# Reordering loads and work at the layer change of a two-layer cached-attention decode kernel, with a rebuilt final projection

## The chip, the cores and the metric

The kernel runs on one core of one Trainium2 chip. The metric is device time in microseconds (us). The kernel before took 547.49 us in the median of its first 4 runs (547.14 to 548.09).

A "page" is the summary of one profiled execution; the other views are answers to questions put to the same trace. Engines: PE is the matrix engine, PEld its weight loads, DVE the vector engine, ACT the scalar engine, POOL the general engine. SP is the engine that issues the loads here, and SPq its queue.

## The reference

One token goes through attention, a gated feed-forward network, and then both again. Both layers have the **same** weights and the same caches.

```
x = A_x                                    # 1 x 1 x 640
x = x + attention(layernorm(x), k_cache, v_cache, wq, wo)
x = x + ffn(layernorm(x), w1, w3, w2)
x = x + attention(layernorm(x), k_cache, v_cache, wq, wo)   # same operands
x = x + ffn(layernorm(x), w1, w3, w2)
# attention: 32 heads of width 192, the last 4096 of 32768 cached positions
# ffn: silu(x w1) * (x w3), then w2; hidden size 1536
```

Nearly everything is reading: per layer, 4096 positions x 192 x 32 heads of K and as much of V in bfloat16 are 100.7 MB, plus 21.6 MB of weights.

## The kernel before

Everything that comes from HBM lands in one large tile, `pg`. It consists of an auxiliary area (columns 0 to 10752) and seven slots of 12288 columns, 3.1 MB each. One slot holds one K or V tile: 2 heads x 4096 positions. The 32 heads are four blocks `b` of four such tiles `z`. A list of loads is planned in advance. `need` issues planned loads up to the wanted one; each waits on SP until its place is free. So **the order of the plan is the order of the stream**, and a load whose place is not free holds up all behind it.

```python
def need(key):
    while key not in place:
        k, at, n, src = queue.pop(0)
        ...                                  # asserts that the place is free by plan
        nc.sync.dma_start(out=pg[:, at:at + n], in_=src)
        place[k] = live[k] = (at, n)
    ...
```

For each block: K is transposed in place on DVE, multiplied with q on PE (scores, `s_ps`), softmax makes `ptm`, V is multiplied (`o_ps`), the result is gathered (`combine`) and multiplied with `wo`. Layer 0 goes through blocks 0, 1, 2, 3, layer 1 backwards, so that block 3's K (four slots) and part of its V (two and a half slots) stay in place from layer 0. At the layer change almost all space is therefore taken, and the next loads depend on how soon it is given back.

```python
# plan at the layer change
for half in (1, 0):                       # wq again, in 10 pieces of 0.79 MB
    for c in range(NCH):
        plan(("wq", 1, half, c), ring(3072), 3072, ...)
plan_k(1, 2, 0, 1)                        # K of block 2, tile 0 -> slot 1
plan_k(1, 2, 1, 3)
plan_v(1, 3, 0, 5)
plan_k(1, 2, 2, 2)
plan_vhalf(1, 3, 3, 0, slot(0))
plan_k(1, 2, 3, 6)                        # -> slot 6, which holds V tile 1 of block 3
plan_cut(("wo", 1, 3), D, (12,), wo_v[3], 0)
...
# work at the head of layer 1
qhalf(1)                                  # q of half the heads, with its copies
build_w(order[0])
for z in range(NZ):
    k_stage(order[0], z, s_ps, ...)       # scores with the K still in place
    if z == 1:
        qhalf(0)                          # the other half, in the middle of the scores
build_w(order[1])
l, et = softmax_front(s_ps)
softmax_back(et)
for bi, b in enumerate(order):
    ...
    for k in range(NZ):
        k_stage(nxt, k, ...)              # transpose + scores of the next block
        v_stage(b, vz[k], ...)            # one V product; vz = 1, 2, 0, 3 in this block
```

The end of the kernel writes the residual as a row with small matmuls and two ACT copies, multiplies with w2 in 24 matmuls on one row of PSUM, and adds twice on DVE:

```python
for f ...:                                # 12 rows of w2
    for nh in range(2):
        nc.tensor.matmul(z_ps[nh][0:1, 0:320], lhsT=otd[:, f:f + 1], rhs=w[:, o:o + 320], ...)
for nh in range(2):
    nc.vector.tensor_tensor(out=ob[:, 320 * nh:...], in0=z_ps[nh][0:1, 0:320], in1=xr[...], op=ALU.add)
nc.sync.dma_start(out=out[0, :, :], in_=ob)
```

Of the kernel before, what the change touches and what calls it, by code (L numbers as in the profile page):

```python
# [16 lines left out]
P = 128  # L17
# [23 lines left out]
CUT_2 = ((4, 4, 4), (6, 4, 2))  # L41

# [7 lines left out]
def kernel(  # L50
# [64 lines left out]
    def plan_v(layer, b, z, s):  # L115
        plan(("v", layer, b, z), slot(s), SLOT, kv_src(A_v_cache, b, z))

    def plan_vhalf(layer, b, z, half, at):
        plan(("v", layer, b, z, half), at, HALF, kv_src(A_v_cache, b, z, TP // 2 * half, TP // 2))
# [37 lines left out]
    plan_vhalf(0, 3, 3, 0, slot(0))  # L157
    plan_vhalf(0, 3, 3, 1, slot(0) + HALF)
    plan_cut(("wo", 0, 3), D, CUT_WO, wo_v[3])
    plan_ffn(0)  # L160
    for half in (1, 0):
        for c in range(NCH):
            o = 6144 * c + 3072 * half
            plan(("wq", 1, half, c), ring(3072), 3072, wq_v[:, o:o + 3072])
    plan_k(1, 2, 0, 1)
    plan_k(1, 2, 1, 3)
    plan_v(1, 3, 0, 5)
    plan_k(1, 2, 2, 2)
    plan_vhalf(1, 3, 3, 0, slot(0))
    plan_k(1, 2, 3, 6)  # L170
    plan_cut(("wo", 1, 3), D, (12,), wo_v[3], 0)
    for (b, ks, vs) in ((2, (1, 3, 2, 6), (4, 5, 0, 1)),
                        (1, (4, 5, 0, 1), (3, 2, 6, 4))):
        for z in range(NZ):
            plan_k(1, b - 1, z, ks[z])
            plan_v(1, b, z, vs[z])
        plan_cut(("wo", 1, b), D, (12,), wo_v[b], 0)
    for z, s in enumerate((3, 5, 2, 0)):
        plan_v(1, 0, z, s)
    plan_cut(("wo", 1, 0), D, CUT_WO, wo_v[0], 0)  # L180
# [147 lines left out]
    def v_values(parts, z, o_ps, first, last):  # L328
        u = 0
        for x in parts:  # L330
            for i in range(x.shape[1] // 384):
# [5 lines left out]
                                 rhs=x[:, 384 * i:384 * i + 384], start=st, stop=(last and u >= 28),  # L337
# [3 lines left out]
    def combine(o_ps, l, first):  # L341
        o_sb = wrk.tile([P, 384], BF16, tag="w0", name="o_sb")
        nc.scalar.copy(out=o_sb[:], in_=o_ps[:, 0:384])  # L343
# [3 lines left out]
        nc.vector.reciprocal(out=rl[:], in_=rl_ps[:])  # L347
        ot_ps = ps_m.tile([P, 16, 12], F32, tag="m", name="ot_ps")
# [7 lines left out]
        o12 = sml.tile([P, 12], F32, tag="o12", name="o12")  # L356
        nc.vector.reduce_sum(out=o12[:], in_=_ap(om[:], 0, P, 0, [[1, 12], [12, 16]]), axis=AX.X)
        if first:
            nc.vector.tensor_copy(out=otp[:, :, 0], in_=o12[:, 0:4])
        nc.vector.tensor_copy(out=otd[:], in_=o12[:])  # L360
# [25 lines left out]
    def ffn_hidden(layer):  # L386
        gu = wrk.tile([P, 2, 384], BF16, tag="w1", name="gu")
        gt_ps = ps_m.tile([P, 2, 3, 4], F32, tag="m", name="gt_ps")
        gu_ps = [ps_a.tile([P, 512], F32, tag="a", name=f"gu_ps{i}") for i in range(2)]
        for gi in range(2):  # L390
            c = 0
            for i, n in enumerate(CUT_1):
# [8 lines left out]
                done(key)  # L401
            if gi == 0:
# [3 lines left out]
        for gi in range(2):  # L406
            for k in range(3):
                nc.tensor.matmul(gt_ps[:, gi, k, :], lhsT=gu[:, gi, k:384:3], rhs=sel4[:], start=True, stop=True)
        ex = sml.tile([P, 12], F32, tag="ex", name="ex")
# [17 lines left out]
    def residual_row():  # L427
        at = slot(3)
        ident = pg[:, at:at + 2 * P].bitcast(F32)
        xr = pg[0:1, at + 2 * P:at + 2 * P + 2 * D].bitcast(F32)  # L430
        selector(ident, [(0, [[-1, P]])])
        r_ps = [ps_a.tile([P, 512], F32, tag="a", name=f"r_ps{i}") for i in range(2)]
        for nh in range(2):
            for c in range(NCH):
                nc.tensor.matmul(r_ps[nh][0:1, 64 * c:64 * c + 64], lhsT=xsq[:, c:c + 1],
                                 rhs=ident[:, 64 * nh:64 * nh + 64], start=True, stop=True)
            nc.scalar.copy(out=_ap(xr, 0, 1, 320 * nh, [[1, NCH], [NCH, 64]]),
                           in_=r_ps[nh][0:1, 0:320].rearrange("p (c k) -> p c k", c=NCH))
        return xr

    def ffn_out(layer, xr):
        z_ps = [ps_a.tile([P, 512], F32, tag="a", name=f"z_ps{i}") for i in range(2)]
        f = 0
        for i, n in enumerate(CUT_2[layer]):
            w = need(("w2", layer, i))
            for fl in range(n):
                for nh in range(2):
                    o = D * fl + 320 * nh
                    nc.tensor.matmul(z_ps[nh][0:1, 0:320], lhsT=otd[:, f:f + 1], rhs=w[:, o:o + 320],  # L449
                                     start=(f == 0), stop=(f == 11))  # L450
                f += 1
        ob = pg[0:1, slot(5):slot(5) + D]
        for nh in range(2):
            nc.vector.tensor_tensor(out=ob[:, 320 * nh:320 * nh + 320], in0=z_ps[nh][0:1, 0:320],
                                    in1=xr[:, 320 * nh:320 * nh + 320], op=ALU.add)
# [8 lines left out]
    for layer in range(2):  # L464
        last_b = 3 if layer == 0 else 0
        order = (0, 1, 2, 3) if layer == 0 else (3, 2, 1, 0)
        if layer == 0:
            q_ps = [ps_a.tile([P, 512], F32, tag="a", name=f"q_ps{i}") for i in range(2)]
# [9 lines left out]
            qproj_tail(q_ps[1], 1)  # L478
        else:
            layernorm()  # L480

        def qhalf(half):
            qh_ps = ps_a.tile([P, 512], F32, tag="a", name="qh_ps")
            for c in range(NCH):
                qproj_mm(qh_ps, half, c, need(("wq", 1, half, c)), 0)
                done(("wq", 1, half, c))
            qproj_tail(qh_ps, half)

        def k_stage(b, z, s_ps, first, last):
            key = ("k", 0 if b == 3 else layer, b, z)  # L490
            xk = need(key)
            if not (layer == 1 and b == 3):
                k_transpose(xk)
            k_scores(xk, z, s_ps, first, last)
# [84 lines left out]
```

## Time and profile before

| what | value | view |
|---|---|---|
| time, median | 547.49 us | runs |
| read from HBM | 224.13 MB | page |
| rate from 24 to 264 us | 429 GB/s | stretches |
| rate from 300 to 384 us | 368 GB/s | stretches |
| PE, DVE busy | 52%, 46% | page |

These are lines of the page of the kernel before. Each row of digits has 40 slices of the span, 13.7 us each; a 9 on the DMA row means 90% busy or more, and GB/s is what the core's DMA engines moved in the slice.

```profile
span 546.4 us, 5551 instructions
...
DMA  8999999999999999999999799599999999999995
GB/s 355 432 429 432 430 427 428 430 430 431 432 428 430 431 429 432 429 430 428 412 401 395 281 421 407 229 431 433 434 426 432 428 432 430 429 426 432 430 405 230
...
HBM read 224.13 MB, written 0.00 MB: 410 GB/s over the span
```

The DMA row is all nines but for the start and three places. The rate sits near 430 GB/s and falls at slices 23 and 26 (281 and 229 GB/s) and in the last (230). PE and DVE are busy about half of the time (table). So the stream bounds the kernel, and what can be gained is the time when it does not run.

Next are stretches of 3 us around the layer change (columns: stretch, its length, busy us and instruction count of PE, PEld, DVE, ACT, POOL, then granted PE clock, DMA share and GB/s; bytes are counted where their packets start).

```profile
core 0: us, PE busy (x) PEld busy (x) DVE busy (x) ACT busy (x) POOL busy (x), PEclk, DMA share, GB/s
306.00:309.00 3.00, 3.00 (x16) 0.90 (x14) 0.00 (x0) 0.00 (x0) 0.00 (x0) 0.50 0.75 305
309.00:312.00 3.00, 3.00 (x16) 0.84 (x14) 0.00 (x0) 0.00 (x0) 0.00 (x0) 0.94 0.06 25
312.00:315.00 3.00, 3.00 (x18) 0.84 (x16) 0.00 (x0) 0.00 (x0) 0.00 (x0) 1.00 0.91 303
345.00:348.00 3.00, 3.00 (x16) 0.87 (x14) 3.00 (x3) 0.00 (x0) 0.00 (x0) 0.68 0.82 336
348.00:351.00 3.00, 3.00 (x40) 1.20 (x38) 3.00 (x2) 0.00 (x0) 0.00 (x0) 1.00 0.00 0
351.00:354.00 3.00, 3.00 (x20) 0.95 (x18) 3.00 (x3) 0.00 (x0) 0.00 (x0) 1.00 0.48 131
```

There are two holes: one around 309 to 312 us, one around 348 to 352 us. PE is fully busy in both: it computes what the stream waits for. The issues of the SP queue say which load ended each hole (start, duration, instruction).

```profile
300.20 2.19 SPq L97 DMA_DIRECT2D pg<-in_A_wq_dram  x2
311.12 5.76 SPq L97 DMA_DIRECT2D pg<-in_A_k_cache_dram  x2
...
332.00 0.55 SPq L97 DMA_DIRECT2D pg<-in_A_v_cache_dram  x1
351.48 0.54 SPq L97 DMA_DIRECT2D pg<-in_A_k_cache_dram  x1
```

After the last wq piece (the second of the two from 300.20) nothing is issued until 311.12, when the scores with the first kept K tile have freed slot 1. After 332.00 nothing is issued until 351.48: slot 6 is freed by the first V product, which stands behind softmax, a K transpose and scores.

The end, in the timeline: the last w3 matmuls, the 24 z matmuls, the adds, the issue of the output.

```profile
536.35 1.49 PE L397 MATMUL gu_ps<-pg,xs 128*32 128x384 bf16 x12 [0.15 <-DMA pg<-in_B_w_dram]
...
539.98 3.42 PE L449 MATMUL z_ps<-pg,otd 128*1 128x320 bf16 x24
543.36 0.95 DVE L454 TENSOR_TENSOR pg<-z_ps,pg 1x320 bf16<-1x320 f32 x2 [3.43 <-PE z_ps L449]
544.34 0.31 SPq L456 DMA_DIRECT2D out_dram<-pg  x1
```

### The profile page before, as it was taken

How to read it: one execution, taken by the hardware profiler on the slowest of the kernel's cores; microseconds unless marked ns; L12 is line 12 of the kernel's file. 1: busy time of each engine (PE TensorE's matmuls, PEld its weight loads, DVE VectorE, ACT ScalarE, POOL GpSimd, SP SyncE). 2: the span in 40 equal slices, each digit the busy share in tenths (PEclk: the TensorE clock that was granted, in tenths of full speed). 3: DMA queues.
4: the chain of work that ended last, by engine and by line, in shares of the span. 5: the costliest groups of instructions: out<-in, count | busy, mean ns of one | idle time of the engine just before them, and what ended most of it. 6: DMA issues, size and time to landing. Idle time of an engine off the chain costs nothing.

```text
span 546.4 us, 5551 instructions
## 1 busy us (share of the span) xinstructions
PE 281.6 (52%) x2407; PEld 104.1 (19%) x2407; DVE 251.4 (46%) x297; ACT 41.1 (8%) x94; POOL 8.6 (2%) x37
## 2 busy tenths in 40 slices
PE   1427627455444444455445782765554545446446
PEld 1201102121111111112122230222111111112123
DVE  2279587445444654442022105964943464443011
ACT  1100020020000200001010002002000100002001
POOL 5000000000000000000000000000000000000000
PEclk9998769775777777675555696897597757768558
DMA  8999999999999999999999799599999999999995
GB/s 355 432 429 432 430 427 428 430 430 431 432 428 430 431 429 432 429 430 428 412 401 395 281 421 407 229 431 433 434 426 432 428 432 430 429 426 432 430 405 230
DMA packets 14859, 224.50 MB, mean 411 GB/s; under 512 B 1777, under 2 KB 1778, under 8 KB 6130
## 3 DMA queue, kind: packets, MB, share of 16 engines
q1 hardware_dynamic: 14690, 224.14, 96.9%
q8 instruction: 19, 0.31, 0.2%
q14 instruction: 6, 0.05, 0.0%
q10 hardware_dynamic: 144, 0.00, 0.0%
HBM read 224.13 MB, written 0.00 MB: 410 GB/s over the span
## 4 chain that ended last, share of the span: by engine, by line
DMA 62%; PE 18%; DVE 16%; issue 2%; ACT 1%; SPq 1%; ACTq 0%; DVEq 0%
DMA pg<-in_A_k_cache_dram 49%; PE s_ps L292 13%; DVE pg L285 11%; DMA pg<-in_A_wo_dram 4%; DMA pg<-in_B_w_dram 4%; DMA pg<-in_A_v_cache_dram 3%; PE o_ps L336 2%; DMA pg<-in_A_wq_dram 2%; ACT e L311 1%; PE y_ps L372 1%; DVE et L315 1%; DVE wst L277 1%; SPq L97 1%; PE z_ps L449 1%; PE qh_ps L253 1%
## 5 line engine op out<-in xcount | busy, mean ns | idle before, releaser
L292 PE MATMUL s_ps<-pg,wst 128*32 128x512 bf16 x768 | 175.2, 619 | 168.6 <-DVE pg L285 167.6
L285 DVE STREAM_TRANSPOSE pg<-pg 128x1536 uint32<-128x1536 uint32 x112 | 188.7, 1745 | 103.7 <-DMA pg<-in_A_k_cache_dram 103.6
L292 PEld LDWEIGHTS <-wst 128*32 128x32 bf16 x768 | 47.0, 117 | 281.5 <-issue 247.8
L336 PE MATMUL o_ps<-pg,ptm 128*16 128x384 bf16 (+1 forms) x1024 | 83.2, 378 | 24.4 <-DMA pg<-in_A_v_cache_dram 24.4
L336 PEld LDWEIGHTS <-ptm 128*16 128x16 bf16 (+1 forms) x1024 | 33.4, 99 | 61.8 <-issue 52.0
L311 ACT ACTIVATE e<-s_ps,nbt 32x512 bf16<-32x512 f32 x16 | 13.1, 820 | 366.6 <-DVE nbt L307 366.4
L277 DVE TENSOR_TENSOR wst<-qt_sb,grp 128x96 bf16<-128x96 bf16 x16 | 8.1, 696 | 39.0 <-PE s_ps L292 38.9
L347 DVE RECIPROCAL rl<-rl_ps 128x1 f32<-128x1 f32 x8 | 1.1, 133 | 48.1 <-PE rl_ps L345 48.1
L372 PE MATMUL y_ps<-pg,otd 128*1 128x320 bf16 x192 | 14.7, 465 | 9.7 <-DVE otd L360 9.1
L315 DVE STREAM_TRANSPOSE et<-e 64x1024 bf16<-64x1024 bf16 x8 | 9.9, 1236 | 15.2 <-ACT e L311 15.2
L324 ACT COPY ptm<-et 32x256 bf16<-32x256 bf16 x32 | 13.4, 420 | 8.0 <-DVE et L315 7.4
L350 PE MATMUL ot_ps<-o_sb,csel 128*128 128x192 bf16 x16 | 3.2, 292 | 17.3 <-ACT o_sb L343 17.0
L264 DVE CAST q_rep<-qh_ps 128x768 bf16<-128x768 f32 x2 | 1.9, 956 | 20.4 <-ACT q_rep L262 20.4
L397 PE MATMUL gu_ps<-pg,xs 128*32 128x384 bf16 x80 | 8.2, 508 | 5.8 <-DMA pg<-in_B_w_dram 2.9
L298 DVE TENSOR_REDUCE t<-s_ps 64x1 f32<-64x512 f32 x8 | 5.1, 637 | 11.5 <-PE s_ps L292 11.5
L253 PE MATMUL q_ps<-pg,xs 128*32 128x384 bf16 x80 | 7.0, 521 | 6.3 <-DMA pg<-in_A_wq_dram 4.9
L326 DVE COPY ptm<-et 32x256 bf16<-32x256 bf16 x32 | 9.2, 286 | 0.6
L253 PEld LDWEIGHTS <-xs 128*32 128x32 bf16 x160 | 6.1, 122 | 15.7 <-issue 10.8
L372 PEld LDWEIGHTS <-otd 128*1 128x1 bf16 x192 | 5.9, 113 | 16.1 <-DVE otd L360 11.1
L253 PE MATMUL qh_ps<-pg,xs 128*32 128x384 bf16 x80 | 6.8, 422 | 3.4 <-DMA pg<-in_A_wq_dram 2.1
L234 PE MATMUL st_ps<-xsq,onesD 128*128 128x12 f32 x8 | 2.3, 367 | 11.4 <-DVE xsq L232 11.4
L200 POOL MEMSET pg<- 128x128 f32 x1 | 0.2, 205 | 492.4 <-PE o_ps L336 492.4
(79 smaller groups left out, 87.3 us busy)
## 6 DMA issues: line engine op xcount, KB each, us to landing
pg<-in_A_k_cache_dram SPq DMA_DIRECT2D x28, 3072.0 KB, 41.5
pg<-in_A_v_cache_dram SPq DMA_DIRECT2D x28, 3072.0 KB, 38.8
pg<-in_A_wo_dram SPq DMA_DIRECT2D x6, 1920.0 KB, 32.8
pg<-in_A_wq_dram SPq DMA_DIRECT2D x10, 768.0 KB, 8.5
pg<-in_A_wq_dram SPq DMA_DIRECT2D x2, 3072.0 KB, 13.8
pg<-in_B_w_dram SPq DMA_DIRECT2D x8, 768.0 KB, 15.9
pg<-in_A_v_cache_dram SPq DMA_DIRECT2D x3, 1536.0 KB, 16.2
pg<-in_A_wo_dram SPq DMA_DIRECT2D x6, 640.0 KB, 22.0
```

Of the source, the lines that this page charges most:

```text
L97: nc.sync.dma_start(out=pg[:, at:at + n], in_=src)
L253: nc.tensor.matmul(q_ps[32 * j:32 * j + 32, 0:384], lhsT=xs4[:, c, c2, :], rhs=w[:, o:o + 384], start=(c == 0 and cl == 0), stop=(c == NCH ...
L277: nc.vector.tensor_tensor(out=_ap(wst[:], 0, P, 4 + 216 * h, [[433, NZ], [36, 6], [8, 4]]), in0=_ap(qt_sb[:], 0, P, 96 * h + 4 * b, [[1, N ...
L285: nc.vector.transpose(v, v)
L292: nc.tensor.matmul(s_ps[32 * h:32 * h + 32, :], lhsT=wst[:, z, h, it, 4 - 4 * th:36 - 4 * th], rhs=_ap(x, 0, P, 192 * th + 64 * be + par + ...
L311: nc.scalar.activation(out=_ap(e[:], 32 * h, 32, h, [[32, 32], [2, 16]]), in_=s_ps[r, :].rearrange("p (t j) -> p t j", j=16), func=ACTF.Ex ...
L315: nc.vector.transpose(et[:], e[:])
L324: nc.scalar.copy(out=dst, in_=src)
L326: nc.vector.tensor_copy(out=dst, in_=src)
L336: nc.tensor.matmul(o_ps[32 * j:32 * j + mw, 0:384], lhsT=ptm[:, po:po + mw], rhs=x[:, 384 * i:384 * i + 384], start=st, stop=(last and u > ...
L372: nc.tensor.matmul(y_ps[nh][32 * j:32 * j + mw, 0:320], lhsT=lhsT, rhs=w[:, o:o + 320], start=st, stop=(last and ci >= 8), tile_position=( ...
L397: nc.tensor.matmul(gu_ps[gi][32 * j:32 * j + 32, 0:384], lhsT=xs4[:, c, 0, :], rhs=_ap(w, 0, P, FF * cl + 3 * j, [[12, 128], [1, 3]]), sta ...
```

## The change

It has four aims. (1) At the layer change, loads that need little are put where the stream was empty: two pieces of `wo` go ahead of the first K. (2) Space is freed sooner: half of q's tail leaves the scores, a K tile is transposed early, and the V products that free slots come before further K transposes. (3) `combine` gets a shorter chain. (4) The final projection uses two column tiles of PE, starts from the residual, copies out on two engines, and has "warm-up" matmuls that compute nothing of use. The diff, cut to its core:

```diff
+CUT_V = (32, 16, 16)          # the last V tile of a layer in three pieces (was two halves in layer 0, one piece in layer 1)
+CUT_WOX = (5, 4, 3)
 # plan at the layer change
+    plan_cut(("wo", 1, 3), D, CUT_WOX[:2], wo_v[3], 0)
     plan_k(1, 2, 0, 1)
-    plan_k(1, 2, 1, 3)
-    plan_v(1, 3, 0, 5)
+    plan_v(1, 3, 0, 3)
+    plan_k(1, 2, 1, 5)
+    plan_v(1, 3, 3, 0, CUT_V, kept=2)
     plan_k(1, 2, 2, 2)
-    plan_vhalf(1, 3, 3, 0, slot(0))
     plan_k(1, 2, 3, 6)
-    plan_cut(("wo", 1, 3), D, (12,), wo_v[3], 0)
+    plan(("wo", 1, 3, 2), 9 * D, 3 * D, wo_v[3][:, 9 * D:12 * D])
 ...
 # head of layer 1
+            q_mms(q_ps[1], 1, range(NCH))
+            qproj_tail(q_ps[1], 1)
+            q_mms(q_ps[0], 0, (0, 1))
+            build_w(order[0])
+            for z, cs in enumerate(((2, 3), (4,), (), ())):
+                k_stage(order[0], z, s_ps, z == 0, z == NZ - 1)
+                q_mms(q_ps[0], 0, cs)
+        k_ready(order[1], 0)                 # transpose ahead of softmax, both layers
         build_w(order[1])
         l, et = softmax_front(s_ps)
+        if layer == 1:
+            k_stage(order[1], 0, s_ps, True, False)
         softmax_back(et)
+        if layer == 1:
+            qproj_tail(q_ps[0], 0)
 ...
+            if layer == 1 and bi == 0:
+                steps = "v1 v2 v0 k1 v3 k2 k3"
+            elif nxt is not None:
+                steps = "k0 v0 k1 v1 k2 v2 k3 v3"
 ...
+                    k_ready(order[bi + 2], 0)   # every block: next K transposed before softmax
 # combine: row sums earlier, copy split over ACT and DVE, one cast dropped
 # end: residual matmuls first (start=True), then
-                    nc.tensor.matmul(z_ps[nh][0:1, 0:320], ..., start=(f == 0), stop=(f == 11))
+                    nc.tensor.matmul(zr[nh], ..., start=False, stop=(f == 11),
+                                     tile_position=(0, 32 * nh), skip_group_check=True)
+        nc.vector.tensor_copy(out=ob[:, 0:320], in_=zr[0])
+        nc.scalar.copy(out=ob[:, 320:640], in_=zr[1])
 # layer 1's ffn: warm(2) after w3's first piece, warm(1) and warm(3) around the gate's transposes
```

More of the change, by code (lines that the diff above doesn't have):

```diff
@@ L113, in plan_k, with plan_v @@
         plan(("k", layer, b, z), slot(s), SLOT, kv_src(A_k_cache, b, z))
-    def plan_v(layer, b, z, s):
-        plan(("v", layer, b, z), slot(s), SLOT, kv_src(A_v_cache, b, z))
-    def plan_vhalf(layer, b, z, half, at):
-        plan(("v", layer, b, z, half), at, HALF, kv_src(A_v_cache, b, z, TP // 2 * half, TP // 2))
+    vkeys = {}
+    def plan_v(layer, b, z, s, cuts=(TP,), kept=0):
+        t = 0
+        keys = vkeys[layer, b, z] = vkeys[0, b, z][len(cuts) - kept:] if kept else []
+        for i, nt in enumerate(cuts[:len(cuts) - kept]):
+            plan(("v", layer, b, z, i), slot(s) + t * DH, nt * DH, kv_src(A_v_cache, b, z, t, nt))
+            keys.insert(i, ("v", layer, b, z, i))
+            t += nt
     ring_at = [0]
@@ L156 @@
     plan_v(0, 3, 2, 4)
-    plan_vhalf(0, 3, 3, 0, slot(0))
-    plan_vhalf(0, 3, 3, 1, slot(0) + HALF)
+    plan_v(0, 3, 3, 0, CUT_V)
     plan_cut(("wo", 0, 3), D, CUT_WO, wo_v[3])
@@ L164 @@
             plan(("wq", 1, half, c), ring(3072), 3072, wq_v[:, o:o + 3072])
+    plan_cut(("wo", 1, 3), D, CUT_WOX[:2], wo_v[3], 0)
     plan_k(1, 2, 0, 1)
-    plan_k(1, 2, 1, 3)
-    plan_v(1, 3, 0, 5)
+    plan_v(1, 3, 0, 3)
+    plan_k(1, 2, 1, 5)
+    plan_v(1, 3, 3, 0, CUT_V, kept=2)
     plan_k(1, 2, 2, 2)
-    plan_vhalf(1, 3, 3, 0, slot(0))
     plan_k(1, 2, 3, 6)
-    plan_cut(("wo", 1, 3), D, (12,), wo_v[3], 0)
-    for (b, ks, vs) in ((2, (1, 3, 2, 6), (4, 5, 0, 1)),
-                        (1, (4, 5, 0, 1), (3, 2, 6, 4))):
+    for z in (1, 2):
+        vkeys[1, 3, z] = list(vkeys[0, 3, z])
+    plan(("wo", 1, 3, 2), 9 * D, 3 * D, wo_v[3][:, 9 * D:12 * D])
+    for (b, ks, vs) in ((2, (1, 3, 0, 6), (4, 5, 2, 1)),
+                        (1, (4, 5, 2, 1), (3, 0, 6, 4))):
         for z in range(NZ):
@@ L177 @@
         plan_cut(("wo", 1, b), D, (12,), wo_v[b], 0)
-    for z, s in enumerate((3, 5, 2, 0)):
+    for z, s in enumerate((3, 5, 0)):
         plan_v(1, 0, z, s)
+    plan_v(1, 0, 3, 2, CUT_V)
     plan_cut(("wo", 1, 0), D, CUT_WO, wo_v[0], 0)
@@ L336, in v_values, with row_sums @@
                 nc.tensor.matmul(o_ps[32 * j:32 * j + mw, 0:384], lhsT=ptm[:, po:po + mw],
-                                 rhs=x[:, 384 * i:384 * i + 384], start=st, stop=(last and u >= 28),
+                                 rhs=x[:, 384 * i:384 * i + 384], start=st, stop=(last and u >= TP // 2 - 4),
                                  tile_position=(0, 32 * j))
                 u += 1
-    def combine(o_ps, l, first):
-        o_sb = wrk.tile([P, 384], BF16, tag="w0", name="o_sb")
-        nc.scalar.copy(out=o_sb[:], in_=o_ps[:, 0:384])
+    def row_sums(l):
         rl_ps = ps_m.tile([P, 1], F32, tag="m", name="rl_ps")
@@ L347, in combine @@
         nc.vector.reciprocal(out=rl[:], in_=rl_ps[:])
+        return rl
+    def combine(o_ps, rl, first):
+        o_sb = wrk.tile([P, 384], BF16, tag="w0", name="o_sb")
+        nc.scalar.copy(out=o_sb[:, 0:192], in_=o_ps[:, 0:192])
+        nc.vector.tensor_copy(out=o_sb[:, 192:384], in_=o_ps[:, 192:384])
         ot_ps = ps_m.tile([P, 16, 12], F32, tag="m", name="ot_ps")
@@ L355, in combine @@
                                        in1=_ap(dsel[:], 0, P, 0, [[1, 16], [0, 12]]), op0=ALU.mult, op1=ALU.mult)
-        o12 = sml.tile([P, 12], F32, tag="o12", name="o12")
-        nc.vector.reduce_sum(out=o12[:], in_=_ap(om[:], 0, P, 0, [[1, 12], [12, 16]]), axis=AX.X)
+        with nc.allow_low_precision("one of the 16 addends is not zero"):
+            nc.vector.reduce_sum(out=otd[:], in_=_ap(om[:], 0, P, 0, [[1, 12], [12, 16]]), axis=AX.X)
         if first:
-            nc.vector.tensor_copy(out=otp[:, :, 0], in_=o12[:, 0:4])
-        nc.vector.tensor_copy(out=otd[:], in_=o12[:])
+            nc.vector.tensor_copy(out=otp[:, :, 0], in_=otd[:, 0:4])
     def rows_times(keys, cuts, y_ps, first, last):
@@ L389, in ffn_hidden, with warm @@
         gu_ps = [ps_a.tile([P, 512], F32, tag="a", name=f"gu_ps{i}") for i in range(2)]
+        warm_ps = ps_s.tile([P, 512], F32, tag="s", name="warm_ps") if layer == 1 else None
+        def warm(count):
+            for _ in range(count if layer == 1 else 0):
+                nc.tensor.matmul(warm_ps[:], lhsT=csel[:, 0, :, :].rearrange("p h q -> p (h q)"),
+                                 rhs=ptm[:, 0:512], start=True, stop=True)
         for gi in range(2):
@@ L401, in ffn_hidden @@
                 done(key)
+                if gi == 1 and i == 0:
+                    warm(2)
             if gi == 0:
@@ L408, in ffn_hidden @@
                 nc.tensor.matmul(gt_ps[:, gi, k, :], lhsT=gu[:, gi, k:384:3], rhs=sel4[:], start=True, stop=True)
+            warm((1, 3)[gi])
         ex = sml.tile([P, 12], F32, tag="ex", name="ex")
@@ L425, in ffn_down, with ffn_out @@
         y_to_residual(y_ps)
-    def residual_row():
+    def ffn_out(layer):
         at = slot(3)
         ident = pg[:, at:at + 2 * P].bitcast(F32)
-        xr = pg[0:1, at + 2 * P:at + 2 * P + 2 * D].bitcast(F32)
         selector(ident, [(0, [[-1, P]])])
-        r_ps = [ps_a.tile([P, 512], F32, tag="a", name=f"r_ps{i}") for i in range(2)]
+        z_ps = [ps_a.tile([P, 512], F32, tag="a", name=f"z_ps{i}") for i in range(2)]
+        zr = [z_ps[nh][32 * nh:32 * nh + 1, 0:320] for nh in range(2)]
         for nh in range(2):
             for c in range(NCH):
-                nc.tensor.matmul(r_ps[nh][0:1, 64 * c:64 * c + 64], lhsT=xsq[:, c:c + 1],
-                                 rhs=ident[:, 64 * nh:64 * nh + 64], start=True, stop=True)
-            nc.scalar.copy(out=_ap(xr, 0, 1, 320 * nh, [[1, NCH], [NCH, 64]]),
-                           in_=r_ps[nh][0:1, 0:320].rearrange("p (c k) -> p c k", c=NCH))
-        return xr
-    def ffn_out(layer, xr):
-        z_ps = [ps_a.tile([P, 512], F32, tag="a", name=f"z_ps{i}") for i in range(2)]
+                nc.tensor.matmul(zr[nh][:, c:320:NCH], lhsT=xsq[:, c:c + 1], rhs=ident[:, 64 * nh:64 * nh + 64],
+                                 start=(c == 0), stop=False, tile_position=(0, 32 * nh), skip_group_check=True)
+        ffn_hidden(layer)
         f = 0
@@ L448, in ffn_out @@
                     o = D * fl + 320 * nh
-                    nc.tensor.matmul(z_ps[nh][0:1, 0:320], lhsT=otd[:, f:f + 1], rhs=w[:, o:o + 320],
-                                     start=(f == 0), stop=(f == 11))
+                    nc.tensor.matmul(zr[nh], lhsT=otd[:, f:f + 1], rhs=w[:, o:o + 320],
+                                     start=False, stop=(f == 11), tile_position=(0, 32 * nh), skip_group_check=True)
                 f += 1
         ob = pg[0:1, slot(5):slot(5) + D]
-        for nh in range(2):
-            nc.vector.tensor_tensor(out=ob[:, 320 * nh:320 * nh + 320], in0=z_ps[nh][0:1, 0:320],
-                                    in1=xr[:, 320 * nh:320 * nh + 320], op=ALU.add)
+        nc.vector.tensor_copy(out=ob[:, 0:320], in_=zr[0])
+        nc.scalar.copy(out=ob[:, 320:640], in_=zr[1])
         nc.sync.dma_start(out=out[0, :, :], in_=ob)
@@ L466, with kkey, k_ready, k_stage @@
         order = (0, 1, 2, 3) if layer == 0 else (3, 2, 1, 0)
+        def kkey(b, z):
+            return ("k", 0 if b == 3 else layer, b, z)
+        def k_ready(b, z):
+            if not (layer == 1 and b == 3):
+                k_transpose(need(kkey(b, z)))
+        def k_stage(b, z, s_ps, first, last):
+            k_scores(need(kkey(b, z)), z, s_ps, first, last)
+            if not (layer == 0 and b == 3):
+                done(kkey(b, z))
+        def v_stage(b, z, o_ps, first, last):
+            keys = vkeys[layer, b, z]
+            v_values([need(k) for k in keys], z, o_ps, first, last)
+            for k in keys:
+                if not (layer == 0 and b == 3 and k in vkeys[1, b, z]):
+                    done(k)
+        def s_tile():
+            return ps_s.tile([P, 512], F32, tag="s", name="s_ps")
+        def q_mms(qh_ps, half, cs):
+            for c in cs:
+                qproj_mm(qh_ps, half, c, need(("wq", 1, half, c)), 0)
+                done(("wq", 1, half, c))
+        q_ps = [ps_a.tile([P, 512], F32, tag="a", name=f"q_ps{i}") for i in range(2)]
+        s_ps = s_tile()
         if layer == 0:
-            q_ps = [ps_a.tile([P, 512], F32, tag="a", name=f"q_ps{i}") for i in range(2)]
             c = 0
@@ L478 @@
             qproj_tail(q_ps[1], 1)
+            build_w(order[0])
+            for z in range(NZ):
+                k_ready(order[0], z)
+                k_stage(order[0], z, s_ps, z == 0, z == NZ - 1)
         else:
             layernorm()
-        def qhalf(half):
-            qh_ps = ps_a.tile([P, 512], F32, tag="a", name="qh_ps")
-            for c in range(NCH):
-                qproj_mm(qh_ps, half, c, need(("wq", 1, half, c)), 0)
-                done(("wq", 1, half, c))
-            qproj_tail(qh_ps, half)
-        def k_stage(b, z, s_ps, first, last):
-            key = ("k", 0 if b == 3 else layer, b, z)
-            xk = need(key)
-            if not (layer == 1 and b == 3):
-                k_transpose(xk)
-            k_scores(xk, z, s_ps, first, last)
-            if not (layer == 0 and b == 3):
-                done(key)
-        def v_stage(b, z, o_ps, first, last):
-            if b == 3 and z == 3:
-                keys = [("v", layer, b, z, 0), ("v", 0, b, z, 1)]
-            else:
-                keys = [("v", 0 if (b == 3 and z in (1, 2)) else layer, b, z)]
-            v_values([need(k) for k in keys], z, o_ps, first, last)
-            for k in keys:
-                if not (layer == 0 and b == 3 and (z in (1, 2) or k[-1:] == (1,) and len(k) == 5)):
-                    done(k)
-        if layer == 1:
-            qhalf(1)
-        build_w(order[0])
-        s_ps = ps_s.tile([P, 512], F32, tag="s", name="s_ps")
-        for z in range(NZ):
-            k_stage(order[0], z, s_ps, z == 0, z == NZ - 1)
-            if layer == 1 and z == 1:
-                qhalf(0)
+            q_mms(q_ps[1], 1, range(NCH))
+            qproj_tail(q_ps[1], 1)
+            q_mms(q_ps[0], 0, (0, 1))
+            build_w(order[0])
+            for z, cs in enumerate(((2, 3), (4,), (), ())):
+                k_stage(order[0], z, s_ps, z == 0, z == NZ - 1)
+                q_mms(q_ps[0], 0, cs)
+        k_ready(order[1], 0)
         build_w(order[1])
         l, et = softmax_front(s_ps)
+        s_ps = s_tile()
+        if layer == 1:
+            k_stage(order[1], 0, s_ps, True, False)
         softmax_back(et)
+        if layer == 1:
+            qproj_tail(q_ps[0], 0)
         y_ps = None
@@ L522 @@
             o_ps = ps_a.tile([P, 512], F32, tag="a", name="o_ps")
-            if nxt is not None:
-                s_ps = ps_s.tile([P, 512], F32, tag="s", name="s_ps")
-            vz = (1, 2, 0, 3) if (layer == 1 and b == 3) else (0, 1, 2, 3)
-            for k in range(NZ):
-                if nxt is not None:
-                    k_stage(nxt, k, s_ps, k == 0, k == NZ - 1)
-                v_stage(b, vz[k], o_ps, k == 0, k == NZ - 1)
+            if layer == 1 and bi == 0:
+                steps = "v1 v2 v0 k1 v3 k2 k3"
+            elif nxt is not None:
+                steps = "k0 v0 k1 v1 k2 v2 k3 v3"
+            else:
+                steps = "v0 v1 v2 v3"
+            steps = steps.split()
+            vz = [int(st[1]) for st in steps if st[0] == "v"]
+            for st in steps:
+                z = int(st[1])
+                if st[0] == "k":
+                    if z > 0:
+                        k_ready(nxt, z)
+                    k_stage(nxt, z, s_ps, z == 0, z == NZ - 1)
+                else:
+                    v_stage(b, z, o_ps, z == vz[0], z == vz[-1])
+                if st == steps[0]:
+                    rl = row_sums(l)
             if nxt is not None:
                 if bi + 2 < NB:
+                    k_ready(order[bi + 2], 0)
                     build_w(order[bi + 2])
-                l2, et = softmax_front(s_ps)
-            combine(o_ps, l, bi == 0)
+                l, et = softmax_front(s_ps)
+                s_ps = s_tile()
+            combine(o_ps, rl, bi == 0)
             if nxt is not None:
                 softmax_back(et)
-                l = l2
             if y_ps is None:
                 y_ps = [ps_a.tile([P, 512], F32, tag="a", name=f"y_ps{i}") for i in range(2)]
-            cuts = CUT_WO if b == last_b else (12,)
+            cuts = CUT_WO if b == last_b else CUT_WOX if (layer == 1 and b == 3) else (12,)
             rows_times([("wo", layer, b, i) for i in range(len(cuts))], cuts, y_ps, bi == 0, bi == NB - 1)
@@ L543 @@
         layernorm()
-        ffn_hidden(layer)
         if layer == 0:
+            ffn_hidden(layer)
             ffn_down(layer)
         else:
-            ffn_out(layer, residual_row())
+            ffn_out(layer)
 _INS = ['A_x', 'A_k_cache', 'A_v_cache', 'A_wq', 'A_wo', 'B_x', 'B_w1', 'B_w3', 'B_w2']
```

## The prediction

It was made from the profile above, the diff and the order of instructions.

> **What bounds the kernel now.** The HBM stream. The page gives 224.1 MB read at a mean 410 GB/s over 546.4 us; stretch sums give 430 GB/s for 60-260 us and for 390-480 us. PE is 52% busy, DVE 46%. The Trainium skill ("DMA: Bandwidth & Descriptors", section "Where 436 GB/s comes from") names a 435 GB/s ceiling of the SBUF ports; the trace agrees (430). 224.1 MB at 430 GB/s take 521 us, so some 25 us are not stream; the page's slices show where: the layer change (281 and 229 GB/s near 300-355 us) and the last slice (230).
>
> Short stretches and the list of DMA issues detail the layer change. Layer 1's wq is in by 308.3 us. The next load needs K slot 1, freed by the first cached K's scores (5.2 us), so it issues at 311.12 and moves bytes from 312.3: 4 us empty. After the V issue at 332.0 nothing issues until 351.48: slot 6 waits behind softmax, a 6.8 us K transpose (DVE), scores and the first V product; 348-351 us moved nothing. From 309 to 384 us 27.4 MB moved, worth 64 us at 430 GB/s; with the hole's start before 309, about 11.5 us are lost.
>
> **What the change does.** Bytes are equal. (a) Two wo pieces (1.47 MB, 3.4 us) go ahead of the first K load, into space freed by two early q chunks. They fill the first hole to about 311.8; K issues near 311.7 (1.5 us of q matmuls precede the scores) and moves near 312.9: about 1 us stays empty. (b) The q tail (2.3 us) leaves the middle of the cached-K scores, and the V products that free slot 6 run before the K transposes, after one already transposed K. I place slot 6's load at 339.5, while the queue has work to about 345.8. The second hole closes. I find no new stall later. (c) The next block's first K transpose moves before softmax and delays it, but issues lead landings by about 40 us, so off the chain. (d) Early row sums, the split copy and the dropped cast shorten each combine by 0.3-0.5 us; only layer 0's end profits, 0.3 us. (e) Tail: the 24 z matmuls (539.98 to 543.36, 143 ns each at full clock) go to two column tiles, estimated 1.7-2 us; two serial 0.48 us output adds become parallel copies: 1.8 us gained. The skill ("TensorE: Matmul & The Clock Gate", section "Part 3: Packing small matmuls") says column tiles run concurrently; this trace agrees: 24 wo matmuls on four tiles took 1.78 us at half clock, 74 ns each.
>
> **Sum.** 11.5 - 1 = 10.5 us at the layer change, 1.8 tail, 0.3 elsewhere: 547.5 - 12.6 = 534.9 us, range 532.5 to 538.0; just past the 2% line (536.5). Faster by over 2%: 0.77; within 2%: 0.225; slower: 0.005.
>
> **What would show it.** Right: between 300 and 380 us only one gap, about 1 us near 312; no long slot-6 wait in the SP queue's waits; z matmuls near 1.8 us; steady stretches still 430 GB/s. Wrong: a second empty stretch at 340-355 us, or a lower stream rate in layer 1.
>
> **What would make it wrong.** The queue running dry later, because the early-transposed K delays softmax and so slot release; smaller pieces streaming slower; the clock staying at half during z (1.5 us more); the first hole not closing, as scores start later.

## More of the kernel before

From the end of the w3 matmuls (537.84) to the output's issue (544.34) are 6.5 us.

## The result, and the profile after

The changed kernel took 536.42 us (median of 8 runs, 536.30 to 538.91) against 547.64 us (13 runs). The ratio is 0.9802, with a 95% interval of 0.9792 to 0.9813. Ratios here are the mean time of one kernel's fast runs over that of the other's of the same rounds, so not quite the ratio of the medians. The gain is 11.2 us, and whether it passes 2% is not settled: the interval holds 0.98.

Lines of the page after:

```profile
span 534.3 us, 5558 instructions
...
DMA  8999999999999999999999999999999999999996
GB/s 355 438 424 431 438 421 431 432 427 434 432 423 425 436 429 434 429 427 433 414 417 409 408 388 435 406 429 437 429 426 430 430 431 431 424 436 430 416 412 272
...
HBM read 224.13 MB, written 0.00 MB: 419 GB/s over the span
```

The dips at slices 23 and 26 are gone (408 and 406 GB/s, with 388 at slice 24 the lowest near them), only the last slice is still low, and the mean rate rose from 410 to 419 GB/s. The bytes are the same. Stretches at the same times as above:

```profile
306.00:309.00 3.00, 3.00 (x16) 1.61 (x14) 0.00 (x0) 0.00 (x0) 0.00 (x0) 0.83 1.01 421
309.00:312.00 3.00, 3.00 (x30) 1.79 (x27) 0.00 (x0) 0.00 (x0) 0.00 (x0) 1.00 0.93 345
312.00:315.00 3.00, 3.00 (x16) 1.51 (x14) 0.00 (x0) 0.00 (x0) 0.00 (x0) 1.00 0.91 348
345.00:348.00 3.00, 1.34 (x6) 0.35 (x7) 1.61 (x1) 0.00 (x0) 0.00 (x0) 0.99 1.03 442
348.00:351.00 3.00, 3.00 (x18) 0.89 (x16) 2.68 (x2) 0.00 (x0) 0.00 (x0) 0.50 1.05 451
351.00:354.00 3.00, 2.62 (x38) 1.04 (x33) 3.00 (x3) 0.00 (x0) 0.00 (x0) 0.94 0.84 358
```

No stretch is empty any more. Around 309 to 315 the stream runs slowly (345 and 348 GB/s); against 430 that loses (85 + 82) x 3 / 430 = 1.2 us. The issues of the SP queue:

```profile
304.77 0.84 SPq L99 DMA_DIRECT2D pg<-in_A_wo_dram  x2
310.58 0.55 SPq L99 DMA_DIRECT2D pg<-in_A_k_cache_dram  x1
...
327.49 12.19 SPq L99 DMA_DIRECT2D pg<-in_A_k_cache_dram  x2
```

The two `wo` pieces issue at 304.77, the first K at 310.58. The last line joins the K load issued at 327.49 with the next one, for slot 6. The timeline shows the latter by itself:

```profile
337.01 2.11 PE L345 MATMUL o_ps<-pg,ptm 128*32 128x384 bf16 x32
339.15 0.53 SPq L99 DMA_DIRECT2D pg<-in_A_k_cache_dram  x1
339.85 6.76 DVE L294 STREAM_TRANSPOSE pg<-pg 128x1536 uint32<-128x1536 uint32 x4
```

The first V product ends at 339.1, slot 6's load issues at 339.15 instead of 351.48, and only then does DVE transpose the next K. The end:

```profile
525.48 1.51 PE L416 MATMUL gu_ps<-pg,xs 128*32 128x384 bf16 x12 [0.47 <-DMA pg<-in_B_w_dram]
...
529.14 0.98 PE L466 MATMUL z_ps<-pg,otd 128*1 128x320 bf16 x12 [0.57 <-DVE otd L439]
530.35 1.23 PE L466 MATMUL z_ps<-pg,otd 128*1 128x320 bf16 x12 [0.23 <-DMA pg<-in_B_w_dram]
531.61 0.48 DVE L470 CAST pg<-z_ps 1x320 bf16<-1x320 f32 x1 [2.52 <-PE z_ps L466]
531.64 0.42 ACT L471 CAST pg<-z_ps 1x320 bf16<-1x320 f32 x1 [3.53 <-PE z_ps L466]
532.15 0.31 SPq L472 DMA_DIRECT2D out_dram<-pg  x1
```

From the end of the w3 matmuls (526.99) to the output's issue (532.15) are 5.2 us, 1.3 us fewer than before. The second half of the z matmuls waited for w2's second piece and started at 530.35. The line merges what follows: in the trace the last four of these twelve waited again, for w2's third piece, and started at 531.14.

**Where the time came from.** The trace has start, duration and size of each packet, so one can ask when a given number of MB had landed. This table has us after the first packet's start on the queue of the loads (packet ends; one profiled run of each kernel; the five other kernels are experiments, described below).

| MB landed | before | after | wo_late | v_late | both_late | order_only | stream_only |
|---|---|---|---|---|---|---|---|
| 110 | 257.65 | 257.47 | 257.44 | 257.41 | 257.69 | 257.32 | 256.55 |
| 128 | 301.58 | 300.76 | 301.02 | 300.79 | 300.95 | 300.82 | 299.36 |
| 132 | 316.07 | 311.93 | 316.08 | 312.14 | 315.97 | 312.13 | 309.20 |
| 144 | 345.31 | 340.78 | 344.61 | 340.85 | 344.27 | 340.89 | 337.27 |
| 150 | 365.66 | 354.77 | 358.61 | 362.32 | 366.17 | 354.82 | 351.26 |
| 200 | 481.93 | 471.15 | 475.03 | 478.76 | 482.77 | 471.25 | 467.27 |
| 224 | 538.76 | 527.97 | 531.89 | 535.51 | 539.53 | 528.12 | 523.54 |

Before minus after is 0.8 us at 128 MB, 4.1 at 132 (the first hole), 4.5 at 144, 10.9 at 150 (the second hole), and then stays: 10.8 at 224. The spans differ by 12.1 us, so 1.3 us come from the end. Nothing was won or lost in the 74 MB after the layer change.

### The profile page after: what moved, and what is told of

It reads as the page before. It is cut to its first block, busy times and chain, and to the rows that moved or that the text cites. A ratio compares the mean times of both kernels' runs of the same rounds, so it can differ in the third digit from the quotient of the medians.

```text
span 534.3 us, 5558 instructions
## 1 busy us (share of the span) xinstructions
PE 285.6 (53%) x2412; PEld 107.2 (20%) x2413; DVE 252.5 (47%) x296; ACT 39.0 (7%) x93; POOL 8.6 (2%) x37
## 4 chain that ended last, share of the span: by engine, by line
DMA 64%; DVE 16%; PE 13%; ACT 3%; issue 3%; SPq 1%; another core or an unknown queue 0%; ACTq 0%; DVEq 0%
DMA pg<-in_A_k_cache_dram 43%; DVE pg L294 10%; DMA pg<-in_B_w_dram 8%; DMA pg<-in_A_v_cache_dram 7%; PE s_ps L301 7%; DMA pg<-in_A_wo_dram 4%; ACT e L320 2%; PE y_ps L384 2%; PE o_ps L345 2%; DVE et L324 2%; DMA pg<-in_A_wq_dram 2%; SPq L99 1%; DVE wst L286 1%; ACT ptm L333 1%; DVE otd L370 0%
## 5 line engine op out<-in xcount | busy, mean ns | idle before, releaser
L301 PEld LDWEIGHTS <-wst 128*32 128x32 bf16 x768 | 52.0, 116 | 215.1 <-issue 189.7
L345 PE MATMUL o_ps<-pg,ptm 128*16 128x384 bf16 (+1 forms) x1024 | 75.2, 379 | 22.0 <-DMA pg<-in_A_v_cache_dram 21.5
L363 PE MATMUL ot_ps<-o_sb,csel 128*128 128x192 bf16 x16 | 5.0, 313 | 68.5 <-ACT o_sb L359 63.2
L345 PEld LDWEIGHTS <-ptm 128*16 128x16 bf16 (+1 forms) x1024 | 30.7, 98 | 54.1 <-issue 43.2
L262 PE MATMUL q_ps<-pg,xs 128*32 128x384 bf16 x160 | 15.7, 490 | 11.5 <-DMA pg<-in_A_wq_dram 10.2
L360 DVE CAST o_sb<-o_ps 128x192 bf16<-128x192 f32 x8 | 2.6, 322 | 37.6 <-ACT o_sb L359 37.6
L363 PEld LDWEIGHTS <-csel 128*128 128x128 bf16 x16 | 1.6, 101 | 66.8 <-issue 66.8
L273 DVE CAST q_rep<-q_ps 128x768 bf16<-128x768 f32 x4 | 3.8, 958 | 20.3 <-ACT q_rep L271 20.3
L262 PEld LDWEIGHTS <-xs 128*32 128x32 bf16 x160 | 6.6, 124 | 17.7 <-issue 11.5
```

Source lines behind the costliest of these rows:

```text
L262: nc.tensor.matmul(q_ps[32 * j:32 * j + 32, 0:384], lhsT=xs4[:, c, c2, :], rhs=w[:, o:o + 384], start=(c == 0 and cl == 0), stop=(c == NCH ...
L301: nc.tensor.matmul(s_ps[32 * h:32 * h + 32, :], lhsT=wst[:, z, h, it, 4 - 4 * th:36 - 4 * th], rhs=_ap(x, 0, P, 192 * th + 64 * be + par + ...
L345: nc.tensor.matmul(o_ps[32 * j:32 * j + mw, 0:384], lhsT=ptm[:, po:po + mw], rhs=x[:, 384 * i:384 * i + 384], start=st, stop=(last and u > ...
L363: nc.tensor.matmul(ot_ps[:].rearrange("p q i -> p (q i)"), lhsT=csel[:, par, :, :].rearrange("p h q -> p (h q)"), rhs=o_sb[:, 192 * par:19 ...
```

## The experiments

My theory: the gain is the stream's two holes at the layer change, plus the end. The rival: the compute chain got shorter (early transposes, shorter combine), and the order of the loads matters little. Differences below are against the median of the changed kernel, 536.42 us; each round also ran the kernel before, whose medians differed by 0.4 us at most. The changed kernel itself was not run again in these rounds, so differences of some tenths of a us are not settled.

### 1. The wo pieces late again

```diff
-    plan_cut(("wo", 1, 3), D, CUT_WOX[:2], wo_v[3], 0)
     plan_k(1, 2, 0, 1)
     ...
     plan_k(1, 2, 3, 6)
     ...
+    plan_cut(("wo", 1, 3), D, CUT_WOX[:2], wo_v[3], 0)
```

> The changed kernel with the two wo pieces moved back behind layer 1's first five K and V loads; all else kept. My theory (the gain is stream holes closed at the layer change): the stream stands empty from the end of wq to the first K, about 4 us instead of about 1, so about 3 us slower than the changed kernel, 539.4 us, and no second hole. Rival (the gain is a shorter compute chain: earlier transposes, shorter combine, so the order of the loads hardly matters): within 0.7 us of 536.4.

Measured: 540.05 us, 3.6 us slower. Two stretches of its trace:

```profile
306.00:309.00 3.00, 3.00 (x17) 1.56 (x14) 0.00 (x0) 0.00 (x0) 0.00 (x0) 0.88 0.62 258
309.00:312.00 3.00, 3.00 (x29) 1.73 (x27) 0.00 (x0) 0.00 (x0) 0.00 (x0) 1.00 0.01 4
```

Where the changed kernel moved 421 and 345 GB/s, this one moved 258 and 4. The table above shows 3.9 us lost at 224 MB, nearly all of it already at 132 MB (4.2). The rival is out for this part: no arithmetic changed, only the place of 1.47 MB in the stream.

### 2. The V products behind a K transpose again

```diff
-                steps = "v1 v2 v0 k1 v3 k2 k3"
+                steps = "k1 v1 v2 v0 k2 v3 k3"
```

> The changed kernel with layer 1's first block ordered K1 before the first V product (k1 v1 v2 v0 k2 v3 k3 instead of v1 v2 v0 k1 v3 k2 k3). My theory: the load into slot 6 issues near 351 instead of near 339.7, the queue is empty from about 345.5 to 352.5, so 6 to 7 us slower, about 543 us. Rival (compute chain): the same work in another order, within 1 us of 536.4.

Measured: 544.27 us, 7.9 us slower. Stretches, and two lines of the timeline:

```profile
345.00:348.00 3.00, 3.00 (x16) 0.87 (x14) 0.00 (x0) 0.00 (x0) 0.00 (x0) 0.68 0.33 139
348.00:351.00 3.00, 3.00 (x36) 1.19 (x36) 0.73 (x2) 0.00 (x0) 0.00 (x0) 1.00 0.00 0
```

```profile
337.72 6.76 DVE L294 STREAM_TRANSPOSE pg<-pg 128x1536 uint32<-128x1536 uint32 x4
350.16 3.69 PEld L345 LDWEIGHTS <-ptm 128*32 128x32 bf16 x96
```

The transpose (6.8 us) and its scores stand ahead of the V product, which starts only at 350.2; the stream has run dry by then. The table shows 7.5 us at 150 MB and the same at 224: what is lost here is never made good, because afterwards the stream is always full.

### 3. Both

> Both of the two edits. If the holes are independent they add: about 9.8 us slower than the changed kernel, 546.2 us, which would be nearly all of the gain at the layer change. If one hole hides in the other (the first delay gives the second wait its time back), about 543 us as with the second alone. Rival (compute chain): within 2 us of 536.4.

Measured: 547.63 us, 11.2 us slower, and equal to the kernel before (ratio 1.0005, 0.9990 to 1.0020). 3.6 + 7.9 = 11.5: the holes add. The sum is larger than I expected because each was. This kernel is not the one before, for it keeps the new end, which is worth 1.3 us; its stream is 0.8 us later than before's at 224 MB, since its second hole is somewhat longer than the old one.

### 4. The old end

The changed kernel with the old residual row, one column tile, two serial adds and no warm-ups.

> The changed kernel with the old end: residual row by separate matmuls and copies, z matmuls on one column tile, two serial adds, no warm-up matmuls. From the two traces (last w3 matmul to output issue 6.5 us before, 5.2 us after) I expect 1.3 us slower, 537.7 us; my prediction had said 1.8. A rival that gives the whole gain to the layer change expects 536.4.

Measured: 538.01 us (537.58 to 538.58), 1.6 us slower. That is between what the traces said (1.3) and what the prediction said (1.8), and its runs scatter too much to choose. Its own trace chooses: from the end of the w3 matmuls (527.32) to the output's issue (533.75) are 6.4 us, 1.3 more than in the changed kernel.

### 5. Without the warm-up matmuls

```diff
-                if gi == 1 and i == 0:
-                    warm(2)
 ...
-            warm((1, 3)[gi])
```

> The changed kernel without its six warm-up matmuls near the end. If they earn the tail's gain: the clock is at 0.5 when the z matmuls run, which then take about twice as long (second half 1.23 us to about 1.8 or more), 0.5 to 1.5 us slower, 537 to 538 us. If column tiles and parallel copies earn it: the clock is up anyway, as it was in the kernel before without any of them, and the time stays within 0.3 us of 536.4.

Measured: 537.63 us (537.16 to 537.83), 1.2 us slower. Two lines of its timeline, and its stretch from 530 to 533:

```profile
529.72 3.36 PE L463 MATMUL z_ps<-pg,otd 128*1 128x320 bf16 x24 [1.24 <-DVE otd L436]
533.66 0.31 SPq L469 DMA_DIRECT2D out_dram<-pg  x1
```

```profile
530.00:533.00 3.00, 3.00 (x24) 1.24 (x20) 0.00 (x0) 0.00 (x0) 0.00 (x0) 0.50 0.14 52
```

The clock is at 0.50 and the 24 z matmuls on two tiles take 3.36 us: as long as 24 on one tile took at full clock before (3.42 us). By the starts of the single matmuls in the traces, a pair on two tiles started every 0.27 us here and every 0.136 us in the changed kernel, at full clock; one matmul on one tile started every 0.136 us in the kernel before. So two tiles doubled the rate at full clock, and half the clock took that gain away. One tile at half the clock was not run.

From the end of the w3 matmuls (527.58) to the output's issue are 6.1 us here, 0.9 more than in the changed kernel: that is what the warm-ups are worth in these two traces. The rest of the difference (1.5 us between the spans) was there before: the last w3 matmuls waited for their load until 526.08 here and until 525.48 there.

The Trainium skill ("TensorE: Matmul & The Clock Gate", section "What's actually happening") says that activity releases a throttle in windows of about 3.4 us. The trace agrees: all granted clocks are 0.5 or 1.0, and they change at multiples of 3.41 us. In the kernel before and in the old end the clock was up during z without any warm-ups. There, 20 small residual matmuls ran just ahead of z; the change moved these to the front. That they had kept the clock up, and that the warm-ups replace them, fits both traces but was not tried by itself. They did not raise it: in the kernel before it rose at 538.06, and the first of them started at 538.67.

### 6. The early K transposes of the other blocks undone

```diff
-                    k_ready(order[bi + 2], 0)      # and k_ready moved back into the block's own loop
```

> The changed kernel with the next block's first K transpose back in its old place, after softmax (kept early only in layer 1's first block, where the loads' order needs it). My theory: off the chain, since loads lead by about 40 us: within 0.5 us of 536.4, with steady stretches still at 430 GB/s. Rival (the early transpose shortens the compute chain of every block by up to 6.8 us and earns the gain): 3 us slower or more.

Measured: 536.74 us (536.67 to 536.76), 0.3 us slower; ratio 0.9805. The rival's 3 us are not there.

### 7. More work in the middle

```diff
+                    if layer == 0 and nxt == 2 and z == 1:
+                        for _ in range(2):
+                            k_transpose(need(kkey(nxt, z)))    # three times is once
```

> The changed kernel with one K tile of layer 0's second block transposed three times in place of once (same result, 13.5 us more of VectorE work in the chain of that block). If the stream has tens of us of slack there: 536.4 within 0.5. If the engines' chain bounds the steady part: up to 13.5 us slower.

Measured: 536.45 us (536.20 to 536.82), no difference. From its page:

```profile
L294 DVE STREAM_TRANSPOSE pg<-pg 128x1536 uint32<-128x1536 uint32 x120 | 202.2, 1746 | 101.2 <-DMA pg<-in_A_k_cache_dram 101.1
```

The added transposes are there (120 in place of 112, DVE at 265.5 us busy instead of 252.5), and they cost nothing. In the steady part the engines have at least 13 us of slack in that block.

### 8. The old combine

Row sums after the V products, one ACT copy, a separate cast.

> The changed kernel with the old combine: row sums after the V products, one 384-column copy on ScalarE, a separate cast. My prediction gave these 0.3 us, at the end of layer 0 only: 536.7 us. If every block's combine counts, 8 x 0.4 us: 539 us. If the stream hides all of it: 536.4.

Measured: 536.91 us (536.49 to 538.04), 0.5 us slower in the median, with a ratio of 0.9814 (0.9800 to 0.9827) whose interval overlaps that of the changed kernel. The 2.6 us of "every block counts" are out. Whether it is 0.3, 0.5 or nothing is not settled.

### 9. What is left when the rest is undone

The old combine, the old end and the old place of the K transposes together; what is left is the order at the layer change and the finer cut of V.

> The changed kernel with the old combine, the old end without warm-up matmuls, and the early K transpose only in layer 1's first block: what is left of the change is the order of loads and of work at the layer change, and the finer V cut. If the parts add, the single runs give 536.4 + 0.5 (combine) + 1.6 (end) + 0.3 (early K) = 538.8 us, so the layer change alone is worth 8.5 us of the 11. If the parts hide one another, 538.0 us; if they need one another, 540 us or more.

Measured: 537.73 us (537.68 to 540.26): 9.7 us faster than the kernel before in the same rounds (547.41 us), and 1.3 us slower than the changed kernel. The small losses of experiments 6 and 8 do not add to that of the end. In the table its stream is within 0.2 us of the changed kernel's throughout, with the old combine. So the combine does not speed the stream up, not even at the end of layer 0.

### 10. The stream alone

All loads in the changed kernel's order, sizes and places, no computing, a wrong result.

> The changed kernel's loads alone, in its order, sizes and places, with no computing (the result is wrong on purpose). This measures the floor of the stream: 224.1 MB at 430 GB/s are 521 us, with the start, the small pieces and the end about 527 to 530 us. If it came out near 536, the changed kernel would have no hole left to close; if near 521, small pieces would cost nothing by themselves.

Measured: 531.01 us. Two lines of its page:

```profile
span 529.3 us, 172 instructions
HBM read 224.13 MB, written 0.00 MB: 423 GB/s over the span
```

This is what these loads cost with no one to wait for; the changed kernel is 5.4 us above it. The last column of the table says where: 1.4 us by 128 MB, 2.7 by 132, 3.5 by 144, 4.4 by 224; the spans differ by 5.0. So of the hole that ended at 132 MB, some 1.3 us are left. The estimate of 527 to 530 us was a little low. Its rate from 264 to 308 us, where the loads are weights with mostly 5 to 6 KB in a row of a partition, is 416 GB/s, against 430 before and after.

### 11 and 12. Two tries at something faster

The end of the ring (1536 columns) is free at the layer change, and a quarter of the first half of V's last tile belongs there. So it can be loaded ahead of the `wo` pieces:

```diff
+    plan(("v", 1, 3, 3, 1), slot(0) + 24 * DH, 8 * DH, kv_src(A_v_cache, 3, 3, 24, 8))
     plan_cut(("wo", 1, 3), D, CUT_WOX[:2], wo_v[3], 0)
```

> A try at something better than the changed kernel: a quarter of the first half of block 3's last V tile (0.39 MB, 0.9 us at 430 GB/s), whose home in the ring's unused end is free at that time, is loaded right after wq, ahead of the two wo pieces, so that the stream has work until the first K can issue. My theory: about 0.9 us of the remaining hole at 310-313 closes, 535.5 us. Rival (that hole is only the slow start of a large transfer): no change, 536.4.

Measured: 537.01 us (536.76 to 537.57), no faster and perhaps 0.6 us slower. The stretch from 309 to 312 us is better than the changed kernel's (371 against 345 GB/s) but that from 306 to 309 is worse (373 against 421): the piece, 3 KB in a row, and the change to it cost about what it was to fill. At 132, 200 and 224 MB the stream is where the changed kernel's is, within 0.3 us. The end is later: by 222.5 MB both streams were equal (524.03 and 524.02 us in the count of the table), yet the last w3 matmuls started at 526.89 here and at 525.48 there. These matmuls need w3's second piece, whose last packet landed at 526.37 here and at 525.01 there, although packets of w2, the next load but one, had started at 523.31 and 523.89. Why the end of one piece lagged 3.1 us behind the start of a later one here, against 1.1 us there, is open; the profiled run was the slowest of the five.

The second try cut layer 1's w2 in two pieces (8 and 4 rows) on top of it.

> The filler kernel with layer 1's w2 loaded in two pieces of 8 and 4 rows in place of 6, 4 and 2. Twelve of the 24 z matmuls wait for the second piece and then take 1.23 us; with 8 rows in the first piece only 8 are left. If the last landing bounds the tail, 0.4 us faster than the filler kernel; if the first, larger piece now lands late and holds up all 24, no faster or 0.5 us slower.

Measured: 537.56 us (537.27 to 538.12), again no faster. Neither try beats the changed kernel.

## Why the prediction was right, and where it was off

**The bound and the mechanism: right.** The stream bounds the kernel, its rate did not change (429 GB/s from 24 to 264 us in both traces), and the gain at the layer change is two holes closed. Experiments 1 to 3 show this, each with arithmetic unchanged, and experiment 9 shows that the order at the layer change (with V's finer cut) gives 9.7 us by itself.

**The sizes.** Predicted were 10.8 us up to the end of the stream; trace against trace it is 10.8. That they agree so well is partly luck: 10.5 was for the layer change, which gave 10.1 (from 128 to 150 MB), and 0.3 was for the combine, where 0.8 came that is not the combine's (below). The first hole gave 3.3 (from 128 to 132 MB), the second 6.4 (from 144 to 150 MB), and 0.8 had come before 128 MB. Slot 6's load was placed at 339.5 and came at 339.15. The first K was placed at 311.7 and came at 310.58. "About 1 us stays empty" was wrong in kind: no stretch is empty, but two run slowly and lose 1.2 us.

**The step that was mis-sized: the tail, 1.8 us.** It measured 1.3 us between the traces and 1.3 us between experiment 9 and the changed kernel. The estimate gave 1.7 to 2 us to the 24 z matmuls as if nothing held them up. They took 0.98 + 0.23 + 1.23 = 2.44 us, so the prediction's own test, "z matmuls near 1.8 us", was not met. Their cost was right: twelve pairs, one every 0.136 us, the last taking 0.3 us, come to 1.8 us (estimate from the starts in the trace). What was left out is the wait for w2. Its second and third piece landed at 529.88 and 530.68 (ends of their last packets), and the first matmuls on them started 0.47 and 0.46 us later, at 530.35 and 531.14. In the kernel before, z was slower and no z matmul waited. I had named the clock as a risk but had not seen that the warm-ups are there for it; without them the end of the changed kernel's trace is 0.9 us longer (experiment 5).

**The rest of the miss.** The spans differ by 12.1 us, the medians by 11.2. The trace that I read my holes from was of a run of 548.09 us, the slowest of its 13; the median is 547.64. The trace after was of a run of 536.31 us, 0.1 below its median, and the remaining 0.3 us are in the offset from span to time (1.7 us before, 2.0 after). So 534.9 + 0.5 (tail) + 0.9 = 536.3, and 536.4 came. A run chosen for its profile can be half a microsecond from the median, and that matters next to a line drawn at 2%: 0.77 for "faster by over 2%" was too sure.

**(c) early K off the chain: right,** by experiments 6 and 7. **(d) 0.3 us from the combine at the end of layer 0: not shown.** The stream is 0.8 us ahead there, but also in experiment 9, which has the old combine. At 128 MB all twelve traces that compute and have the finer V cut, of the changed kernel and of experiments 1 to 9, 11 and 12, lie between 300.76 and 301.04 us, against 301.58 in the one trace of the kernel before. The finer V cut fits this but was not undone by itself, and one trace before is not enough to rule out the difference of two runs.

**A test that I chose badly.** "No long slot-6 wait in the SP queue's waits" did not hold: the issue before slot 6's was at 327.49, so SP still waited some 11 us. It does no harm, because the loads already issued keep the stream busy. What has to be read is the stream's rate, not the issuer's wait.

## What to carry to other kernels

In a kernel bound by its stream, look for the stretches in which no bytes move and ask for each which load ends it and which place that load waits for; the remedy is a load that needs little ahead of it, or the work that frees the place ahead of other work. What is lost in a hole is never made good where the stream is full, and work added where it is full costs nothing (13 us here). Near the end, where nothing overlaps, check when the last loads land and which clock the last matmuls run at before counting on a faster form of them.

## What the Trainium skill lacked or had wrong

- "DMA: Bandwidth & Descriptors", section "Latency and other measured facts", gives some 600 ns to the first byte of a load issued from SP or ACT. With the queue empty, the first packet started 1.33 to 1.35 us after the start of the issue instruction (issues at 311.12 and 351.48 before and at 310.93 in experiment 1); the instruction itself takes 0.54 us of that.
- The same page, section "Bandwidth", has rates by transfer size for another issuing path. For a full queue of loads issued from SP no page compares lengths of the row in a partition: the stream alone ran at 416 GB/s from 264 to 308 us (mostly 5 to 6 KB) and at 430 GB/s from 24 to 264 us (24 KB for most). These loads also differ in size, so that the row is the cause is not shown.
- "TensorE: Matmul & The Clock Gate", section "Measured speedup vs the span model", has three column tiles and more, but no measurement of two. Two tiles with one column of weights each, at full clock: a pair of matmuls of 320 columns started every 0.136 us, and on one tile a single one every 0.136 us, so two tiles gave twice the rate while nothing held them up.
- No page gives a number for how far the end of one piece can lag behind the packets of a later one on a full queue: the last packet of w3's second piece landed 1.1 us after the first packet of w2 had started in the changed kernel and 3.1 us after it in experiment 11, where the piece was used 1.4 us later with equal bytes landed.
